# A one-layer block with dilated local attention and a gated ReLU network: the second norm only centred, its factor moved to the output rows, and some work moved between engines under a new order

## The chip, the cores and the metric

The kernel runs on one core of a Trainium2 chip. A core has a matrix engine (PE in the profile; its weight loads are PEld), a vector engine (DVE), a scalar engine (ACT), a general engine (POOL) and a synchronising engine that here only starts transfers (SP). PE writes its results into eight PSUM banks of 128 x 512 fp32; ACT or DVE must read a bank before PE can use it for something else. Transfers run on 16 shared DMA engines; SP, ACT and POOL only issue them.

The metric is the device time of one execution in microseconds (us). The kernel before takes 196.03 us (median of three runs, 195.43 to 196.18).

## The reference

The input x has 2048 rows of 512 numbers, in bf16. Two residual steps are computed:

```python
h  = x + attention(layernorm(x)) @ wo          # 32 heads of 16; each row sees itself and the rows
                                               # 2, 4, ..., 14 before it (8 places, dilation 2)
h2 = h + (relu(n @ W_gate) * (n @ W_up)) @ W_down      where n = layernorm(h)
```

The layer norm has no learned factor or offset: it subtracts the row's mean and divides by sqrt(variance + 1e-5). W_gate and W_up are 512 x 1376, W_down is 1376 x 512. ReLU of a row times a positive number is that number times the ReLU, so a positive factor s on a row n comes out of the gated product as s * s.

## The kernel before, in words

The 2048 rows are worked in four chunks of 512 (`tk` 0 to 3), each of four blocks of 128 rows (`j` or `n`). For every chunk the same steps are recorded as operations with an engine, a duration, the operations they depend on and the buffers they take or use:

- First norm (`layernorm` without `residual`): statistics on DVE (`xst`, `xag`), the factor on ACT (`xrl`, `xre`), normalised rows (`xxn`), then a transposition, since PE contracts over partitions: on PE with an ACT copy out of PSUM (`xtp`, `xte`), or, for the pairs of blocks named in `DMAT`, by a transposing DMA issued from SP (`xtd`, line 521).
- Projections (`qkv0` to `qkv11`, line 573): q, k and v in four tiles each, each four matmuls of 512 columns and one ACT copy out of PSUM (line 581). Six of chunk 0's are cut in smaller pieces (`qka` to `qke`) to start with the first rows.
- Scores: q times k at eight shifts, on DVE (`pr`, lines 624 and 639), in two halves `hf` of four shifts. PE sums over the 16 numbers of a head (`sc`, line 630: 16 matmuls that fill a quarter of the array each). For the halves in `PRE` DVE first adds the two products (`pa`, line 667) and PE does 8 matmuls instead of 16 (line 674). ACT takes the exponential (`ex`); the denominators come from PE (`den`), for the chunks in `DEN1` after DVE has added the two halves (`es`, line 720), else as two matmuls (line 708). ACT makes the reciprocal by Ln and Exp (`dl`, `dr`, lines 711 and 714) and DVE multiplies (`am`, line 732).
- SP spreads the weights over partitions with eight broadcasts per chunk (`bd`, line 748), DVE multiplies with v (`mu`, lines 780 and 795) and the eight places are added in three steps (`ta`, `tree`, line 783). The first and largest step is a DMA that adds, issued from POOL (line 823), for the pairs of chunk and tile in `DACC`, else it is done on DVE. `om` or the last step writes the attention output.
- Output projection `wo` (line 861). For the chunks in `RPE` (chunk 0) PE also adds x by a matmul with the identity (line 864) and ACT writes h and its row sum (`rs`, line 870); for the others DVE adds (`rs`, line 872).
- Second norm (`layernorm` with `residual`): DVE makes the negative mean (`hnm`, line 449); ACT makes the sum of squares (`hsq`, line 457), waits for all four blocks, then Ln and Exp (`hrl`, `hre`); only then DVE writes the normalised rows (`hxn`, line 503), which are transposed (`htp` and `hte`, or `htd` by DMA).
- The gated network: gate and up products (`mm`, line 934, and line 901 for the last 96 of 1376 columns), evicted by ACT (`ue`, `ge`) and multiplied on DVE (`gu`); the product with W_down (`dn`, line 984); its rows leave PSUM through ACT for chunks 0 and 1 (`o`, line 993), after which a DMA from POOL adds them to h (`oa`, line 1018), or through DVE, which adds h itself, for chunks 2 and 3 (`o`, line 997). SP stores the rows (`os`).

The order on every engine is fixed in the program. It comes from the list `RANK`: one rank for every operation, in the sequence in which they are recorded. Each engine, and with it the queue of transfers that it issues, works its own operations by rank; a planner (`Plan.order`) only merges these queues and picks buffers, with guessed durations. So an operation that waits holds up all that stands behind it on the same engine. Two weight loads are issued late: W_up after chunk 0's attention (`ldu`), W_down (`ldd`) after chunk 1's broadcasts. `DMAT`, `DACC`, `DEN1`, `PRE` and `RPE` are the lists that decide which engine does what.

Of the kernel before, what the change touches and what calls it, by code (L numbers as in the profile page):

```python
# [8 lines left out]
P = 128  # L9
# [47 lines left out]
]  # L57


class Op:  # L60
# [142 lines left out]
def kernel(  # L203
# [162 lines left out]

    PESUM = ()

    DACC = tuple((k, t) for k in range(3) for t in range(4))
    DAL = 5.5  # L370
    DAC2 = ()
    PRS, MUH = (0,), (0,)
# [698 lines left out]
```

## Time and profile before

| what | before |
|---|---|
| device time, median of three runs | 196.03 us (195.43 to 196.18) |
| profiled execution: time from its first to its last instruction | 193.3 us |
| PE busy | 188.5 us, 98% of the span |
| DVE busy | 149.1 us, 77% |
| ACT busy | 117.9 us, 61% |
| POOL busy | 18.1 us, 9% |
| granted PE clock | 1.000 |
| DMA | 24.61 MB, mean 127 GB/s |

The profiled execution's own time is its span, 193.3 us; the device times of the runs contain 2.7 us more at the median (196.03 - 193.3), which lies before the first and after the last instruction that the profile shows. Durations of instructions come from this one execution. Matmuls are pipelined: the duration of one is longer than the spacing of two, so times on PE are read from groups that follow each other without a break.

### The profile page before, as it was taken

The numbers are of one execution on the slowest core, as the hardware profiler recorded it, in microseconds if no ns is written. First come the engines' busy times: TensorE is split into PE (matmuls) and PEld (weight loads), VectorE is DVE, ScalarE is ACT, GpSimd is POOL, SyncE is SP. The second block draws the span as 40 slices with busy tenths as digits, with TensorE's granted clock in tenths as the row PEclk, the third lists the DMA queues.
The fourth block names the chain that finished last, engine by engine and source line by source line (L and its number), as shares of the span: only waits on it lengthen the run. The fifth ranks groups of instructions, "written<-read, shape, count | busy, mean of one in ns | idle before, by whom it ended". The sixth has DMA issues, their size and how long they took to land.

```text
span 193.3 us, 3095 instructions
## 1 busy us (share of the span) xinstructions
PE 188.5 (98%) x1141; PEld 98.0 (51%) x1141; DVE 149.1 (77%) x238; ACT 117.9 (61%) x245; POOL 18.1 (9%) x32
## 2 busy tenths in 40 slices
PE   7999998999999999999999999999999999999994
PEld 7985453554445443554455444444445445544543
DVE  6899999999899999999998847899965421314232
ACT  3589989887898667572465569505559611276300
POOL 3000003300400013200034101003000000000000
PEclk9999999999999999999999999999999999999999
DMA  6996284991257918947459987221400250170004
GB/s 204 326 353 279 59 191 97 201 201 22 79 213 178 301 33 163 191 84 165 106 111 188 190 171 159 59 54 32 80 0 0 54 136 4 27 244 0 0 4 135
DMA packets 25214, 24.61 MB, mean 127 GB/s; under 512 B 11408, under 2 KB 21488, under 8 KB 25200
## 3 DMA queue, kind: packets, MB, share of 16 engines
q1 hardware_dynamic: 22176, 16.13, 29.7%
q0 software_dynamic: 2304, 7.34, 20.5%
q10 hardware_dynamic: 720, 0.95, 1.5%
q8 instruction: 9, 0.15, 0.3%
q14 instruction: 5, 0.04, 0.1%
HBM read 8.42 MB, written 2.10 MB: 54 GB/s over the span
## 4 chain that ended last, share of the span: by engine, by line
PE 81%; DVE 7%; DMA 6%; ACT 1%; SPq 1%; issue 1%; ACTq 0%
PE bank L934 36%; PE bank L984 20%; PE bank L573 11%; PE bank L861 7%; DVE big L639 4%; PE bank L901 3%; PE bank L630 3%; DVE st L468 3%; DMA x_sm<-in_A_x_dram 2%; DMA wqk_sb<-in_A_wqkv_dram 2%; DMA quad<-row 1%; PE bank L532 1%; DMA big<-ex 1%; SPq L748 1%; ACT kT L581 0%
## 5 line engine op out<-in xcount | busy, mean ns | idle before, releaser
L934 PE MATMUL bank<-quad,wgu_sb 128*128 128x512 bf16 x320 | 71.9, 379 | 0.0
L934 PEld LDWEIGHTS <-wgu_sb 128*128 128x128 bf16 x320 | 31.0, 98 | 36.7 <-issue 0.8
L984 PE MATMUL bank<-wd_sb,gT 128*128 128x512 bf16 (+3 forms) x198 | 39.7, 355 | 0.0
L938 ACT CAST up_sb<-bank 128x512 bf16<-128x512 f32 x40 | 22.4, 592 | 20.7 <-PE bank L934 15.0
L941 ACT ACTIVATE gr<-bank 128x512 bf16<-128x512 f32 x40 | 23.2, 608 | 13.0 <-PE bank L934 9.8
L573 PE MATMUL bank<-quad,wqk_sb 128*128 128x512 bf16 (+2 forms) x176 | 29.9, 321 | 0.8 <-DMA quad<-row 0.8
L984 PEld LDWEIGHTS <-gT 128*128 128x128 bf16 (+1 forms) x198 | 18.4, 98 | 19.6 <-issue 0.4
L624 DVE TENSOR_TENSOR big<-quad,kT 128x4096 bf16<-128x4096 bf16 x12 | 27.2, 2283 | 0.1
L780 DVE TENSOR_TENSOR big<-big,vT 128x4096 bf16<-128x4096 bf16 x12 | 27.0, 2285 | 0.0
L962 DVE TENSOR_TENSOR gT<-gr,up_sb 128x1024 bf16<-128x1024 bf16 x20 | 13.7, 687 | 15.1 <-ACT gr L941 8.7
L573 PEld LDWEIGHTS <-wqk_sb 128*128 128x128 bf16 x176 | 17.1, 113 | 11.5 <-issue 1.4
L823 POOL DMA_DIRECT2D big<-big x12 | 10.5, 884 | 79.6 <-DVE big L780 47.2
L783 DVE TENSOR_TENSOR big<-big 128x1024 bf16<-128x1024 bf16 (+2 forms) x24 | 17.0, 729 | 0.6 <-DMA big<-big 0.5
L573 PE MATMUL bank<-quad,wv_sb 128*128 128x512 bf16 x64 | 15.9, 380 | 0.0
L861 PE MATMUL bank<-wo_sb,quad 128*128 128x512 bf16 x64 | 15.3, 379 | 0.0
L997 DVE TENSOR_TENSOR row<-x_sm,bank 128x512 bf16<-128x512 bf16 (+2 forms) x10 | 5.5, 578 | 12.4 <-PE bank L984 12.4
L457 ACT ACTIVATE row<-x_sm,mv 128x512 bf16<-128x512 bf16 x12 | 8.6, 715 | 4.5 <-DVE mv L449 4.5
L548 ACT COPY quad<-bank 128x1024 bf16<-128x1024 bf16 (+1 forms) x10 | 8.5, 890 | 3.5 <-PE bank L532 3.5
L872 DVE SCALAR_TENSOR_TENSOR x_sm<-x_sm,bank 128x512 bf16<-128x512 bf16 x12 | 8.2, 687 | 3.0 <-PE bank L861 3.0
L468 DVE BATCH_NORM_STATS2 st<-x_sm 128x6 f32<-128x512 bf16 x16 | 10.3, 678 | 0.2 <-DMA x_sm<-in_A_x_dram 0.2
L581 ACT CAST kT<-bank 128x512 bf16<-128x512 f32 x16 | 9.4, 600 | 1.4 <-PE bank L573 0.8
L573 PEld LDWEIGHTS <-wv_sb 128*128 128x128 bf16 x64 | 6.8, 114 | 6.4 <-issue 1.3
(77 smaller groups left out, 173.9 us busy)
## 6 DMA issues: line engine op xcount, KB each, us to landing
big<-big POOLq DMA_DIRECT2D x12, 512.0 KB, 5.3
big<-ex SPq DMA_DIRECT2D x32, 128.0 KB, 2.7
wgu_sb<-in_B_W_gate_dram SPq DMA_DIRECT2D x2, 688.0 KB, 9.9
wgu_sb<-in_B_W_up_dram SPq DMA_DIRECT2D x2, 688.0 KB, 4.7
wd_sb<-in_B_W_down_dram SPq DMA_DIRECT2D x2, 640.0 KB, 5.5
x_sm<-in_A_x_dram SPq DMA_DIRECT2D x2, 512.0 KB, 6.7
x_sm<-up_sb POOLq DMA_DIRECT2D x4, 256.0 KB, 4.5
out_dram<-x_sm SPq DMA_DIRECT2D x4, 256.0 KB, 2.3
```

The costliest lines, as they stand in the source:

```text
L468: V.bn_stats(out=st.t[:], in_=x_sm[:, tk * BPC + j, :])
L573: nc.tensor.matmul(mm.t[:, lo:hi], lhsT=wv_sb[:, dt, t:D:NT] if c == 2 else wqk_sb[:, dt, c * D + t:(c + 1) * D:NT], rhs=xnT.t[:, dt, lo:h ...
L624: V.tensor_tensor(out=pb.t[:].rearrange("p (t w) s -> p t w s", t=2), in0=q4, in1=k4, op=ALU.mult)
L780: V.tensor_tensor(out=mt.t[:], in0=ab.t[:], in1=v8, op=ALU.mult)
L783: V.tensor_tensor(out=mt.t[:, 0:n, :], in0=mt.t[:, 0:n, :], in1=mt.t[:, n:2 * n, :], op=ALU.add)
L823: nc.gpsimd.dma_start(mt.t[:, 0:4, :], mt.t[:, 4:8, :], accum_op=ALU.add)
L861: nc.tensor.matmul(od.t[:], lhsT=OT.t[:, t, j * P:(j + 1) * P], rhs=wo_sb[:, t, :], start=(t == 0), stop=(t == NT - 1 and tk not in RPE))
L934: nc.tensor.matmul(mm.t[:fs, lo:hi], lhsT=wgu_sb[:, dt, g, ft * P: ft * P + fs], rhs=hnT.t[:, dt, lo:hi], start=(dt == 0), stop=(dt == NT ...
L938: nc.scalar.copy(out=ub.t[:fs, i, :], in_=um.t[:fs, :])
L941: nc.scalar.activation(out=gr.t[:fs, i, :], in_=gm.t[:fs, :], func=ACT.Relu)
L962: V.tensor_tensor(out=gt.t[:fs, 0:n, :], in0=gr.t[:fs, 0:n, :], in1=ub.t[:fs, 0:n, :], op=ALU.mult)
L984: nc.tensor.matmul(od.t[:, c0:c1], lhsT=gts[ft].t[:fs, ft % 2, j * P:(j + 1) * P], rhs=wd_sb[:fs, ft, c0:c1], start=(ft == 0), stop=(ft == ...
```

## The change

The second norm is only centred. `hxn` writes h minus its mean as soon as the mean is known and no longer waits for `hsq`, `hrl` and `hre`. The exponent of `hre` becomes -1 instead of -1/2, so that it gives 1 / (variance + eps), the square of the former factor, in buffers of its own (`iv`). That number is applied to the rows at the end: in chunks 0 and 1 as the scale of ACT's copy out of PSUM, in chunks 2 and 3 as the scalar of DVE's multiply-and-add. The squares of `hsq`, of which only the sum is used, go to a scratch tile (`junk`).

Beside that: chunk 0's residual moves from PE and ACT to DVE (`RPE` is empty). Chunk 0's two halves of exponentials are added on DVE before the denominators (`DEN1`). Chunk 3's second half of scores is added in pairs on DVE as well (`PRE`). The first step of the sum over places becomes a DMA for three of chunk 3's four tiles (`DACC`). The second half of chunk 1's second norm is transposed by DMA too (`DMAT`). Ln of the denominators is written back into its PSUM bank instead of a buffer in SBUF. Once the last q and k projections are done, the tile of their weights serves as a sixth large buffer (`big`). All ranks are new, so that the order on every engine is another.

In the new order, by engine (`name.chunk`): SP's queue is `bd0.0 bd1.0 xtd.3 x4 ldu x2 bd1.1 bd0.1 ldd(second part).1 bd1.2 ldd(first part) bd0.2 gtd.0 htd.1 x4 ...`, where before it had `ldd` in both parts straight after chunk 1's broadcasts; PE does chunk 3's first projection straight after `den.0` and chunk 2's four `xtp` later, four `wo.1` before all `dn.0`, and `sc1.2` straight after `sc0.2` behind three `mm.0`.

```diff
-    DEN1 = (1, 2, 3)
+    DEN1 = (0, 1, 2, 3)
-    PRE = ((3,0),)
+    PRE = ((3,0),(3,1))
+    qkb = Buf(big_s)
+    wqk_f = wqk_sb[:].rearrange("p t (w s) -> p (t w) s", s=CS)
-    ln_s = slots(1, [P, CS], F32, "lnd")
+    iv_s = slots(4, [P, BPC], F32, "iv")
+    junk = sb.tile([P, CS], BF16, name="junk")
+    big_s.tiles.insert(0, wqk_f)
-    DACC = tuple((k, t) for k in range(3) for t in range(4))
+    DACC = tuple((k, t) for k in range(3) for t in range(4)) + ((3, 0), (3, 1), (3, 2))
-    DMAT = (('h',2,0),('h',2,2),('h',3,0),('h',3,2),('h',1,0),('x',3,0),('x',3,2))
+    DMAT = (('h',2,0),('h',2,2),('h',3,0),('h',3,2),('h',1,0),('h',1,2),('x',3,0),('x',3,2))
-    RPE, OPE = (0,), ()
+    RPE, POW = (), ()
...
-                        nc.scalar.activation(out=xn.t[:], in_=h.t[:] if h else x_sm[:, tk * BPC + j, :],
+                        nc.scalar.activation(out=junk[:], in_=h.t[:] if h else x_sm[:, tk * BPC + j, :],
                                              func=ACT.Square,
...
                 nc.scalar.activation(out=rs.t[:, lo:hi], in_=rs.t[:, lo:hi], func=ACT.Exp,
-                                     scale=-0.5)
+                                     scale=-1.0 if residual else -0.5)
...
+                elif residual:
+                    V.tensor_scalar(out=xn.t[:], in0=x, scalar1=mv.t[:, j, 0:1], scalar2=None, op0=ALU.add)
...
+                d, u = ([nms[j]], [mv]) if residual else ([e], [nb, rs] if on_act else [mv, rs])
...
-            nc.scalar.activation(out=ld.t[:], in_=dn.t[:], func=ACT.Ln)
+            nc.scalar.activation(out=dn.t[:], in_=dn.t[:], func=ACT.Ln)
...
-                    nc.scalar.copy(out=ob.t[:, j % 2, :], in_=od.t[:])
+                    nc.scalar.activation(out=ob.t[:, j % 2, :], in_=od.t[:], func=ACT.Identity, scale=iv.t[:, j:j + 1])
...
-                    V.tensor_tensor(out=ob.t[:, c0:c1], in0=x_sm[:, tk * BPC + j, c0:c1],
-                                    in1=od.t[:, c0:c1], op=ALU.add)
+                    V.scalar_tensor_tensor(out=ob.t[:, c0:c1], in0=od.t[:, c0:c1], scalar=iv.t[:, j:j + 1],
+                                           in1=x_sm[:, tk * BPC + j, c0:c1], op0=ALU.mult, op1=ALU.add)
```

More of the change, by code (lines that the diff above doesn't have):

```diff
@@ L416 @@
         wload[n] = []
+    wload["q"][0].take.append(qkb)
+    qkb.left += 1
     wb = Buf(bank_s)
@@ L491, in f_nb, with f_pw @@
                                        in1=rs.t[:, lo:hi], op0=ALU.mult, op1=ALU.mult)
-            l = add((ln + "rl" + gk, tk), "ACT", AS, f_ln, ag, pr, take=[rs], use=[sq or mv], lat=AL)
-            e = add((ln + "re" + gk, tk), "ACT", AS, f_ex, [l], pr, use=[rs], lat=AL)
-            if on_act:
+            def f_pw(lo=lo, hi=hi):
+                V.tensor_scalar(out=rs.t[:, lo:hi], in0=mv.t[:, lo:hi, 1], scalar1=EPS, scalar2=-0.5,
+                                op0=ALU.add, op1=ALU.pow)
+            if not residual and tk in POW:
+                e = add((ln + "pw" + gk, tk), "DVE", DSM, f_pw, ag, pr, take=[rs], use=[mv], lat=DL)
+            else:
+                l = add((ln + "rl" + gk, tk), "ACT", AS, f_ln, ag, pr, take=[rs], use=[sq or mv], lat=AL)
+                e = add((ln + "re" + gk, tk), "ACT", AS, f_ex, [l], pr, use=[rs], lat=AL)
+            if residual:
+                ivd.append(e)
+            elif on_act:
                 e = add((ln + "nb" + gk, tk), "DVE", DSM, f_nb, [e], pr, take=[nb], use=[mv, rs], lat=DL)
@@ L498, in f_xn @@
                 x = x_sm[:, tk * BPC + j, :]
-                if on_act:
+                if residual and on_act:
+                    nc.scalar.activation(out=xn.t[:], in_=x, func=ACT.Identity, bias=mv.t[:, j, 0:1], scale=1.0)
+                elif residual:
+                    V.tensor_scalar(out=xn.t[:], in0=x, scalar1=mv.t[:, j, 0:1], scalar2=None, op0=ALU.add)
+                elif on_act:
                     nc.scalar.activation(out=xn.t[:], in_=x, func=ACT.Identity,
@@ L708, in f_dn, with f_ld, f_rc @@
                 nc.tensor.matmul(dn.t[:], lhsT=(same if tk in EARLY else spread)[:], rhs=exs[hf].t[:], start=(hf == 0), stop=(hf == 1))
-        def f_ld(dn=dn, ld=ld):
-            nc.scalar.activation(out=ld.t[:], in_=dn.t[:], func=ACT.Ln)
-        def f_rc(ld=ld, rc=rc):
-            nc.scalar.activation(out=rc.t[:], in_=ld.t[:], func=ACT.Exp, scale=-1.0)
+        def f_ld(dn=dn):
+            nc.scalar.activation(out=dn.t[:], in_=dn.t[:], func=ACT.Ln)
+        def f_rc(dn=dn, rc=rc):
+            nc.scalar.activation(out=rc.t[:], in_=dn.t[:], func=ACT.Exp, scale=-1.0)
         if tk in DEN1:
@@ L725 @@
             b = add(("den", tk), "PE", 2 * MM, f_dn, exd, apr + 2, take=[dn], use=exs, lat=PEL)
-        b = add(("dl", tk), "ACT", A5, f_ld, [b], apr + 2, take=[ld], use=[dn], lat=AL)
-        rcd = add(("dr", tk), "ACT", A5, f_rc, [b], apr + 2, take=[rc], use=[ld], lat=AL)
+        b = add(("dl", tk), "ACT", A5, f_ld, [b], apr + 2, use=[dn], lat=AL)
+        rcd = add(("dr", tk), "ACT", A5, f_rc, [b], apr + 2, take=[rc], use=[dn], lat=AL)
         if tk in EARLY:
@@ L985, in f_dn, with f_o @@
                                      rhs=wd_sb[:fs, ft, c0:c1], start=(ft == 0),
[L986 to L991 removed]
+                                     stop=(ft == NFT - 1))
+            def f_o(j=j, c0=c0, c1=c1, od=od, ob=ob, tk=tk, iv=iv):
                 if tk in ODA:
[L993 to L998 removed]
+                    nc.scalar.activation(out=ob.t[:, j % 2, :], in_=od.t[:], func=ACT.Identity, scale=iv.t[:, j:j + 1])
+                else:
+                    V.scalar_tensor_tensor(out=ob.t[:, c0:c1], in0=od.t[:, c0:c1], scalar=iv.t[:, j:j + 1],
+                                           in1=x_sm[:, tk * BPC + j, c0:c1], op0=ALU.mult, op1=ALU.add)
             last = tk == NCK - 1 and n == len(parts) - 1
@@ L1006 @@
             for lo, hi in ((0, 8), (8, NFT)):
-                a = add(("dn%d" % n, tk), "PE", (hi - lo + (hi == NFT and tk in OPE)) * MM * share,
+                a = add(("dn%d" % n, tk), "PE", (hi - lo) * MM * share,
                         lambda lo=lo, hi=hi, f=f_dn: f(range(lo, hi)),
@@ L1011 @@
             if tk in ODA:
-                b = add(("o%d" % n, tk), "ACT", A5, f_o, [a], mb - 200, take=[ob], use=[od, ob], lat=AL)
+                b = add(("o%d" % n, tk), "ACT", A5 + 0.09, f_o, [a] + ivd, mb - 200, take=[ob], use=[od, ob, iv], lat=AL)
                 if j % 2 == 0:
@@ L1025 @@
                 continue
-            b = add(("o%d" % n, tk), "ACT" if tk in OPE else "DVE", D5 * share + (0.05 if share < 1 else 0), f_o, [a], mb - 200,
-                    take=[ob], use=[od], lat=DL)
+            b = add(("o%d" % n, tk), "DVE", D5 * share + (0.05 if share < 1 else 0), f_o, [a] + ivd, mb - 200,
+                    take=[ob], use=[od, iv], lat=DL)
             add(("os%d" % n, tk), "ACT" if last else "SP", 0.4, f_os, [b], mb + 6, use=[ob], lat=0.55, dq=(0.3, 0.4 * share))
```

42 lines of the change are left out of this document (17 added, 25 removed), and 76 rows, old and new, of the table RANK.

## The prediction

> **What bounds the kernel now.** I read the page, then the waits of PE, then the chain that ended last, then busy times by stretch, and last groups and timelines for single durations.
>
> ```profile
> span 193.3 us, 3095 instructions
> ...
> PE 188.5 (98%) x1141; PEld 98.0 (51%) x1141; DVE 149.1 (77%) x238; ACT 117.9 (61%) x245; POOL 18.1 (9%) x32
> ...
> PE   7999998999999999999999999999999999999994
> ```
>
> PE is busy in every slice. A busy PE need not work at its peak, so the waits say more. These are all waits of PE that the trace names:
>
> ```profile
> PE bank L422 <- DVE warm L322: 1.0, 1, 1.0
> PE bank L573 <- DMA quad<-row: 0.8, 1, 0.8
> ```
>
> The first is the start. The second is the only hole in the middle. The chain shows where it ends and what the work costs behind it (start, duration, what):
>
> ```profile
> 30.85 2.60 DMA quad<-row
> 33.45 0.14 issue
> 33.59 2.75 PE bank L573 x12
> ...
> 38.74 6.04 PE bank L573 x28
> 44.78 0.98 PE bank L630 x16
> ...
> 50.20 0.22 PE bank L864
> ...
> 60.37 0.89 PE bank L532 x16
> ...
> 73.57 0.55 PE bank L674 x8
> ...
> 81.34 0.66 PE bank L901 x8
> ...
> 87.84 3.45 PE bank L861 x16
> ...
> 180.87 9.59 PE bank L984 x66
> 190.46 0.02 issue
> 190.48 0.29 DVE row L997
> ```
>
> From 33.59 to 190.46 the chain holds nothing but matmuls, so there a matmul less is worth its spacing: 6.04 / 28 = 0.216 us for 512 columns, 0.89 / 16 = 0.056 for a transposition. A projection or a gate or up product (four matmuls) is 0.863, a score half 0.98, one added in pairs 0.55. After PE come 2.8 us of last row and store (193.3 - 190.5).
>
> DVE is nearly as full in the middle (columns: stretch, length, then busy time and count of PE, PEld, DVE, ACT, POOL):
>
> ```profile
> 34.00:60.00 26.00, 26.00 (x164) 12.65 (x163) 25.03 (x31) 22.19 (x49) 3.91 (x3) 1.00 0.62 142
> 60.00:80.00 20.00, 20.00 (x122) 9.27 (x121) 20.00 (x14) 12.71 (x24) 3.44 (x4) 1.00 0.72 174
> 80.00:100.00 20.00, 20.00 (x126) 10.04 (x124) 19.73 (x36) 11.83 (x27) 0.86 (x1) 1.00 0.56 117
> ```
>
> So PE sets the end as long as DVE hands it work in time: 64.8 us busy of 66 from 34 to 100.
>
> **What PE loses.** Behind 33.59: four identity matmuls of chunk 0's residual, 4 x 0.216 = 0.86; chunk 3's second score half, 0.98 - 0.55 = 0.43; eight transpositions of chunk 1, 8 x 0.056 = 0.45. Ahead of 33.59: one of chunk 0's two denominator matmuls, 0.22. The last is worth nothing: at the hole PE waits for the transposed rows of chunk 3, and these stand on SP's queue behind chunk 0's eight broadcasts, which start when DVE has ended its eight products, in both orders:
>
> ```profile
> 20.96 5.76 SPq L748 DMA_DIRECT2D big<-ex  x8
> ```
>
> Against that saving, chunk 2's first four transpositions, done ahead of that hole before, now stand behind it: +0.22. Sum: -0.86 - 0.43 - 0.45 + 0.22 = -1.52.
>
> In front of the hole the new order asks `sc0.0` after six of the eight products. By the row below these end at 12.82 + 5 x 1.147 = 18.6, and PE reaches it at about 18.1 (where `sc` stood before, less one transposition); the next, `sc1.0`, needs the eighth product, 20.85. I count 0.8 of new waits. PE had 0.8 to spare at the hole and gains 0.22, so they vanish in it; without that cover they would cost 0.6.
>
> ```profile
> 12.82 8.03 DVE L639 TENSOR_TENSOR big<-quad,kT 128x2048 bf16<-128x2048 bf16 x7
> ...
> 56.23 0.76 DVE L732 TENSOR_TENSOR ex<-ex,rec 128x512 bf16<-128x512 bf16 x2
> ...
> 60.47 6.68 DVE L624 TENSOR_TENSOR big<-quad,kT 128x4096 bf16<-128x4096 bf16 x3
> ...
> 69.28 4.50 DVE L780 TENSOR_TENSOR big<-big,vT 128x4096 bf16<-128x4096 bf16 x2
> ```
>
> **What the others gain and lose.** The groups, with busy time, mean ns of one, and the idle time ahead of them:
>
> ```profile
> L962 DVE TENSOR_TENSOR gT<-gr,up_sb 128x1024 bf16<-128x1024 bf16 x20 | 13.7, 687 | 15.1 <-ACT gr L941 8.7 <-ACT up_sb L938 6.3
> ...
> L500 ACT ACTIVATE row<-x_sm,nb,rs 128x512 bf16<-128x512 bf16 x12 | 9.4, 817 | 0.3 <-DVE nb L489 0.3
> ...
> L872 DVE SCALAR_TENSOR_TENSOR x_sm<-x_sm,bank 128x512 bf16<-128x512 bf16 x12 | 8.2, 687 | 3.0 <-PE bank L861 3.0
> ...
> L783 DVE TENSOR_TENSOR big<-big 128x2048 bf16<-128x2048 bf16 x4 | 4.8, 1220 | 0.0
> ...
> L993 ACT CAST up_sb<-bank 128x512 bf16<-128x512 f32 x8 | 4.4, 599 | 7.4 <-PE bank L984 7.4
> ...
> L870 ACT ACTIVATE x_sm<-bank 128x512 bf16<-128x512 f32 x4 | 2.4, 594 | 0.3 <-PE bank L864 0.3
> ...
> L667 DVE TENSOR_TENSOR big<-big,big 128x4096 bf16<-128x4096 bf16 x1 | 2.3, 2281 | 0.0
> ...
> L720 DVE TENSOR_TENSOR row<-ex,ex 128x512 bf16<-128x512 bf16 x3 | 1.2, 417 | 0.0
> ```
>
> DVE: +4 x 0.69 (chunk 0's residual), +0.42 (`es.0`), +2.28 (pairs), -3 x 1.22 (three first steps of chunk 3 sent to POOL), together +1.8; the output rows that now multiply and add cost what line 872 does, 0.69, and lie beside PE's work but for the last one, 0.29 long. The +3.2 of chunk 0 come early, in the full stretch; the relief comes behind 120. ACT loses 4 x 0.6 and scales eight output rows, 0.60 each now; the new price lies between the same (a scale is free) and the 0.82 of line 500, which scales from SBUF, so 0 to 1.8 in all. I take 0.8, half-way; any of it is hidden in its 39% of idle time, 7.4 us of it ahead of those very rows. Ln into PSUM I price at nothing: same instruction, same input; its bank is held one operation longer. The shorter norm (squares, Ln and Exp out of the path) I also price at nothing: PE waited for no norm after the hole. It pays for DVE's extra work.
>
> **Where the new order can stall: chunk 1.** On PE, from 33.59: 24 projections 20.7, four `xtp` 0.9, two scores 1.96, four `wo.0` 3.45, `den` 0.22, four `htp` 0.89, so the first gate product stands at 61.7, and with 0.1 lost at each change to the scores 61.9. Then 20 gate and up products and two short ones (17.3 + 1.3), two scores, `den.2`: `wo.1` at 82.7, and behind its four `dn.0` at 86.2.
>
> DVE: `am0.1` ended at 56.99 before. Now it has 0.42 and 2.76 and the four centred rows (1.3) more ahead of it, one product (2.2) less, and a wait of 0.65 gone: 58.6. Then four score products (6.68 / 3 = 2.2 each), four products with v (2.2 each), `es.2`, one `gu`, one first sum and `am1.2`: 17.6 + 0.4 + 0.7 + 0.6 + 0.4 = 19.7, which gives `am1.2` at 78.3. Two `gu` and the other sums of chunk 1, 4.4, give the last attention row at 82.7: exactly when PE wants it. Each us that DVE is later here, PE waits. I take 0, half-way between a margin of 0.3 and a wait of 0.3.
>
> At `am1.2` hangs a step that was moved on SP's queue: the first part of W_down, issued before with its second part at 62, now stands behind `bd1.2`, which waits for `am1.2`.
>
> ```profile
> 57.07 5.12 SPq L748 DMA_DIRECT2D big<-ex  x8
> ...
> 62.24 1.22 SPq L304 DMA_DIRECT2D wd_sb<-in_B_W_down_dram  x2
> ...
> 109.51 4.25 SPq L748 DMA_DIRECT2D big<-ex  x4
> ```
>
> ```profile
> big<-big POOLq DMA_DIRECT2D x12, 512.0 KB, 5.3
> ...
> wd_sb<-in_B_W_down_dram SPq DMA_DIRECT2D x2, 640.0 KB, 5.5
> ```
>
> Four broadcasts take 5.12 / 2 = 2.6, so W_down's part goes out at 80.9 and lands at 86.4, against `dn.0` at 86.2: 0.2 late. Lower bound 0 (it lands earlier with the queues empty); upper bound 1.9, if the broadcasts take the 4.25 of the row at 109.51, which ran beside adding transfers. Chunk 1's last adding transfer is issued at about 75.2 and lands at 80.5, so most of its time lies ahead. I take 0.3.
>
> The four transposing DMAs of chunk 1 are issued from 89 on, 1.3 apart, after `rs.1`, and land at 95.6; PE needs them at 96.4. Hidden; the cover is the 9.5 us of `dn.0`. Other handoffs that I added up the same way (chunk 2's output projection at 115, its norm at 128, chunk 3's at 145 and 159) have 0.4 to 3 us.
>
> **Sum.** 193.3 - 1.52 + 0.3 = 192.1, which is -1.2. The profiled execution lies 2.7 below the median, all of it outside the span, so -1.2 is taken from 196.03: 194.8 us.
>
> **A rule against the value of a matmul less.** Four matmuls of 512 columns follow each other every 0.216 us here. The Trainium skill, "TensorE: Matmul & The Clock Gate", section Back-to-back issue gap, states about 131 ns per matmul of 512 columns and 81 ns for 128 as what a real kernel sustains. By it the residual and the transpositions would be worth an estimated 0.52 and 0.65 in place of 0.86 and 0.45, nearly the same sum. The trace disagrees with both figures (0.216 and 0.056), and I go by the trace.
>
> **The rivals.**
>
> (a) The new waits eat most of it: W_down lands 1.9 late, or DVE is 0.5 late at `wo.1` and W_down 1.0 late. About 193.3 - 1.5 + 1.6 = 193.4, so 196.1. For it: two handoffs of margin near zero at 82.7 and 86.2. Against: the order before had as full a DVE and PE did not wait once behind 33.59. Chance 0.22.
>
> (b) On the other side, DVE becomes the bound between 50 and 83: it gets 3.2 us there while it is already 98% busy, and PE has filler only to 82.7. Price: one to one. It decides against the kernel (over +0.5%, 197.0) from 2.2 us of lateness on, beside W_down's 0.3: 197.3 at 2.5. Against: the sums above must be 2.5 short over 25 us of DVE time. Chance 0.11.
>
> (c) Chunk 3's adding transfers hold up DVE. They stand behind the output additions `oa.1` on POOL, which wait for ACT's rows at 129 and 130; landing 5.3 after issue plus the shared time of the output addition, the tree starts at about 137, `gu3.2` behind it at 140, and PE, with all eight banks full, would stop at 141.5. If each landing came 2.2 later, 1 us is lost: 195.8. For 2.2: POOL's issue held by the DVE product that runs. Against: POOL issued one in 0.86 inside the DVE row at 69.28, as here:
>
> ```profile
> 71.87 0.86 POOL L823 DMA_DIRECT2D big<-big  x1 [21.29 <-DVE big L780]
> ```
>
> The Trainium skill, "SBUF — State Buffer", section A bandwidth-pool intuition that's wrong, states that a DMA issued from POOL waits for its descriptors until a DVE instruction that holds the shared port has ended. The row shows no such wait for these products. Chance 0.05.
>
> **How the numbers follow.** Likeliest: PE's saving with small waits, 0.62, 194.8; its own range is 194.3 (no wait) to 195.0. (a) 0.22, (b) 0.11, (c) 0.05. The measurement tells about 0.5%, 1.0 us, from no change: faster is below 195.05, slower above 197.0. Faster 0.62, same 0.27 (a and c), slower 0.11. The range reaches from 194.0 to 196.6: it holds the likeliest, (a) and (c), and leaves out (b) and the tails.
>
> **What would show it.** Right: no line 864 on PE; a pair of scores more in line 674's counterpart; PE's only waits at 18 to 33 and near 83 to 87; PE's last matmul at 189.2. W_down's wait would stand as PE waiting for a DMA into `wd_sb`, (b) as PE waiting for attention rows (`quad` from DVE) at 83, (c) as DVE waiting for `big<-big` at 132 to 140 and PE for ACT at 141. The forecast is wrong if a wait stands at another handoff, or if the hole at 33 ends much later, since all behind it shifts with it.

## The result, and the profile after

The changed kernel takes 195.19 us (median of 16 runs, 193.94 to 196.07), the kernel before 195.62 (16 runs, 195.06 to 196.18): ratio 0.9966, 95% interval 0.995 to 0.9982. Two later comparisons gave 0.9952 and 0.9962. So it is faster by 0.34%, about 0.7 us (the two medians alone differ by 0.43), where 1.2 us were forecast, and less than the 0.5% above which I had called it faster. The profiled execution took 195.59, 0.4 above the median. For 212 runs of the kernels below both the time and the span of the same execution were measured: the time is 1.7 to 2.25 us longer than the span. So the profile of the kernel before, with a span of 193.3, is of an execution of some 195.0 to 195.5, and not all of the 2.7 us that I put outside the span lies there.

First the page of the changed kernel: its span, and busy time, share and instructions of each engine.

```profile
span 193.6 us, 3051 instructions
...
PE 185.8 (96%) x1120; PEld 95.9 (50%) x1120; DVE 150.2 (78%) x245; ACT 115.8 (60%) x236; POOL 22.9 (12%) x35
```

PE is busy for 2.7 us less than before, and yet the span of this execution is 0.3 longer. The waits of PE (total, times, longest):

```profile
PE bank L550 <- DVE row L521: 2.2, 2, 1.9
PE bank L429 <- DVE warm L327: 1.0, 1, 1.0
PE bank L591 <- DMA quad<-row: 0.9, 1, 0.9
PE bank L723 <- DVE row L738: 0.4, 1, 0.4
```

All four lie ahead of or in the hole. None of the waits that I had feared behind it is there. The chain (start, duration, what) shows the same handoffs as the forecast, all later by one amount:

```profile
32.40 2.61 DMA quad<-row
35.01 0.14 issue
35.15 5.34 PE bank L591 x24
...
63.65 2.59 PE bank L952 x12
...
84.40 3.45 PE bank L879 x16
87.85 8.86 PE bank L1002 x41
```

The hole ends at 35.15, before at 33.59: 1.56 later. Less this, the first gate product stands at 62.09 (forecast 61.9), `wo.1` at 82.84 (82.7) and `dn.0` at 86.29 (86.2). The part of W_down that `dn.0` needs landed at 87.48, 0.37 ahead of it. At the end, the timeline of the changed kernel:

```profile
183.80 6.49 PE L1002 MATMUL bank<-wd_sb,gT 128*128 128x512 bf16 x47
...
187.29 3.81 SPq L1016 DMA_DIRECT2D out_dram<-row  x6
188.44 1.41 DVE L1010 SCALAR_TENSOR_TENSOR row<-bank,iv,x_sm 128x512 bf16<-128x512 f32 x2 [0.52 <-PE bank L1002]
190.13 0.61 DVE L1010 SCALAR_TENSOR_TENSOR row<-bank,iv,x_sm 128x128 bf16<-128x128 f32 x2 [0.28 <-DMA out_dram<-row]
190.51 0.35 ACTq L1016 DMA_DIRECT2D out_dram<-row  x1
```

PE's last matmul ends at 183.80 + 6.49 = 190.29, so from the hole's end PE needs 155.14; before it was 190.45 - 33.59 = 156.86. PE's saving is 1.72. But the last rows of DVE wait 0.28 for a store (the bracket in their row), and the span ends 3.3 behind the last matmul, where it was 2.8. So 1.72 were won between two points, and 1.56 lost ahead of them and 0.46 behind.

### The profile page after: what moved, and what is told of

Read it like the earlier page. It is cut to its first block, busy times and chain, and to the rows that moved or that the text cites. A ratio compares the mean times of both kernels' runs of the same rounds, so it can differ in the third digit from the quotient of the medians.

```text
span 193.6 us, 3051 instructions
## 1 busy us (share of the span) xinstructions
PE 185.8 (96%) x1120; PEld 95.9 (50%) x1120; DVE 150.2 (78%) x245; ACT 115.8 (60%) x236; POOL 22.9 (12%) x35
## 4 chain that ended last, share of the span: by engine, by line
PE 82%; DMA 7%; ACT 5%; issue 2%; DVE 1%; SPq 0%; DVEq 0%
PE bank L952 35%; PE bank L591 16%; PE bank L1002 15%; PE bank L879 7%; PE bank L648 3%; DMA x_sm<-in_A_x_dram 3%; DMA quad<-row 3%; PE bank L919 3%; PE bank L550 2%; ACT vT L599 1%; DMA out_dram<-row 1%; ACT junk L462 1%; ACT row L518 1%; DVE row L1010 1%; ACT gr L959 1%
## 5 line engine op out<-in xcount | busy, mean ns | idle before, releaser
L642 DVE TENSOR_TENSOR big<-quad,kT 128x4096 bf16<-128x4096 bf16 x11 | 24.9, 2289 | 0.1
L798 DVE TENSOR_TENSOR big<-big,vT 128x4096 bf16<-128x4096 bf16 x10 | 22.5, 2289 | 0.5 <-DMA big<-ex 0.5
L841 POOL DMA_DIRECT2D big<-big x13 | 12.5, 985 | 63.8 <-DVE nb L494 31.6
L1008 ACT ACTIVATE up_sb<-bank,iv 128x512 bf16<-128x512 f32 x8 | 5.1, 684 | 16.3 <-PE bank L1002 16.3
L801 DVE TENSOR_TENSOR big<-big 128x1024 bf16<-128x1024 bf16 (+2 forms) x19 | 12.1, 660 | 3.4 <-DMA big<-big 3.3
L890 DVE SCALAR_TENSOR_TENSOR x_sm<-x_sm,bank 128x512 bf16<-128x512 bf16 x16 | 10.7, 683 | 3.0 <-PE bank L879 3.0
L462 ACT ACTIVATE junk<-x_sm,mv 128x512 bf16<-128x512 bf16 x16 | 11.7, 731 | 1.5 <-DVE mv L456 1.5
L813 DVE TENSOR_TENSOR big<-big,vT 128x2048 bf16<-128x2048 bf16 x8 | 9.3, 1219 | 1.4 <-DMA big<-ex 1.4
L599 ACT CAST quad<-bank 128x512 bf16<-128x512 f32 x16 | 9.1, 590 | 2.1 <-PE bank L591 2.1
L518 ACT ACTIVATE row<-x_sm,nb,rs 128x512 bf16<-128x512 bf16 x12 | 9.8, 815 | 0.3 <-DVE nb L494 0.3
```

Of the source, the lines that this page charges most:

```text
L462: nc.scalar.activation(out=junk[:], in_=h.t[:] if h else x_sm[:, tk * BPC + j, :], func=ACT.Square, bias=mv.t[:, j, 0:1], scale=1.0, accum ...
L642: V.tensor_tensor(out=pb.t[:].rearrange("p (t w) s -> p t w s", t=2), in0=q4, in1=k4, op=ALU.mult)
L798: V.tensor_tensor(out=mt.t[:], in0=ab.t[:], in1=v8, op=ALU.mult)
L801: V.tensor_tensor(out=mt.t[:, 0:n, :], in0=mt.t[:, 0:n, :], in1=mt.t[:, n:2 * n, :], op=ALU.add)
L841: nc.gpsimd.dma_start(mt.t[:, 0:4, :], mt.t[:, 4:8, :], accum_op=ALU.add)
```

## The experiments

The first theories were these. I: the input's blocks land at other times in each execution, and the hole follows. S: the new start order, that of the first operations on DVE and ACT, makes the hole later by 0.5 at any landing. W: waits behind the hole. F came up after the first four runs and is told there.

**The same two kernels again** (labels "changed again" and "before again" in the table below).

> The changed kernel as it is, once more. Theory I (input): in its profiled execution the input rows merely landed late (fourth block at 7.19 us, last block of chunk 1 at 10.30, against 5.91 and 9.40 before), and everything up to the hole at 33 us shifted with them. Then the end of the hole, where the first projection of chunk 3 starts on PE (35.15 there), follows the landing of chunk 1's last block in any execution: landing near 9.4 gives a hole that ends near 33.8 and a span near 191.9. Theory S (start order): the new order of the first rows on DVE, in which block 1 is written only after block 3 has landed, costs about 0.5 us at any landing: the hole ends at 34.3 or later even with a landing at 9.4. Both: PE has no wait over 0.3 us behind the hole.

> The kernel before, once more, for its landings. Theory I: the landing of chunk 1's last input block (9.40 us before) and the end of the hole on PE (33.59) move from execution to execution by 0.5 us or more, and together. Theory S: they stay within 0.2 us, so that the later hole belongs to the new order.

The changed kernel took 194.81 (7 runs), ratio 0.9952 (0.9927 to 0.9977); the one run of the kernel before 194.81, which is low for it (22 runs, 194.63 to 196.38, median 195.64). In both profiles the last input block of chunk 1, for whose statistics DVE's first score products wait, landed at about the same time, 9.19 and 9.15 us, so theory I does not explain what differs. SP's timeline, changed again:

```profile
20.83 6.65 SPq L766 DMA_DIRECT2D big<-ex  x8
27.58 5.25 SPq L539 DMA_TRANSPOSE quad<-row  x4
```

and before again:

```profile
20.70 5.69 SPq L748 DMA_DIRECT2D big<-ex  x8
26.49 5.25 SPq L521 DMA_TRANSPOSE quad<-row  x4
```

SP starts together, but needs 0.96 more to issue the same eight broadcasts. One of the issues takes 1.97 in place of some 0.6 (1.08 before). The first broadcast lands 4.19 after its issue, in the kernel before 3.26. What stands between: a transfer of another kind among the broadcasts' packets. The transfers that started between 22.2 and 22.4 in this profile of the changed kernel (packets, MB, share of 16 engines):

```profile
q1 hardware_dynamic: 20, 0.02, 66.6%
q8 instruction: 1, 0.02, 47.5%
```

The program itself is fetched by such transfers, nine of 16 KB on this queue. Counting PE's weight loads (one for each matmul) in the traces, the second one comes after 212 to 222 of them and the ninth after 1095 to 1100, in every kernel run here; so I take them for PE's, and their time follows PE's progress. Those between scatter more, the fourth from 459 to 497. Each takes about 1 us (0.9 to 1.6). In the kernel before the second one starts at 21.74 and 21.95, ahead of the broadcasts' first packets; in the changed kernel at 22.23 and 23.28, among them. The ninth starts at 184.05 and 184.32 before, where nothing else is under way, and at 187.06 and 187.90 in the changed kernel, where the last rows are stored: it has 21 matmuls with 21 weight loads less, so the same count comes nearer to the end. Changed again, the end of its timeline:

```profile
183.72 5.63 PE L1002 MATMUL bank<-wd_sb,gT 128*128 128x512 bf16 x43
...
186.34 4.42 SPq L1016 DMA_DIRECT2D out_dram<-row  x6
187.50 1.41 DVE L1010 SCALAR_TENSOR_TENSOR row<-bank,iv,x_sm 128x512 bf16<-128x512 f32 x2 [0.52 <-PE bank L1002]
189.80 0.61 DVE L1010 SCALAR_TENSOR_TENSOR row<-bank,iv,x_sm 128x128 bf16<-128x128 f32 x2 [0.89 <-DMA out_dram<-row]
190.18 0.35 ACTq L1016 DMA_DIRECT2D out_dram<-row  x1
```

before again:

```profile
183.70 6.49 PE L984 MATMUL bank<-wd_sb,gT 128*128 128x512 bf16 x47
...
187.33 3.19 SPq L1003 DMA_DIRECT2D out_dram<-row  x6
...
190.23 0.29 DVE L997 TENSOR_TENSOR row<-x_sm,bank 128x128 bf16<-128x128 bf16 x1 [0.33 <-PE bank L984]
190.55 0.36 ACTq L1003 DMA_DIRECT2D out_dram<-row  x1
```

PE ended at 189.35, 0.84 ahead of the kernel before (190.19), close to the forecast (189.2). But DVE's last rows waited 0.89 for the first of the stores, whose row buffer they need: it landed 3.33 after its issue, before 1.71. This is **theory F**: two of PE's instruction transfers now meet transfers on which the hole and the end depend, the second one later than before and the ninth for the first time.

**Start order.** The changed kernel with the old order of DVE's, ACT's and PE's first operations, by permuting ranks:

```diff
+_order(19, 20, 27, 28, 23, 35, 31, 36, 42, 43, 34, 39, 46)   # DVE: xst0 xag0 xst1 xag1 xxn0 xst2 xxn1 xag2 xst3 ...
+_order(21, 22, 29, 30, 26, 37, 38, 44, 45, 41, 48)           # ACT
+_order(24, 25, 32, 33, 67, 61, 77, 72, 55, 68, 73, 40, 78, 47, 74)   # PE
```

> The changed kernel, with the first rows in the order of the kernel before: on DVE block 1 is written ahead of block 3's statistics, ACT's factors to match, on PE the transpositions of blocks 2 and 3 behind the first pieces of the projections. Theory S: the hole ends about 0.5 us earlier than in the changed kernel at the same landing, and the median falls by 0.5 us (ratio to before about 0.994). Theory I: no difference, median within 0.2 us of the changed kernel's (0.9966).

195.2 us, ratio 0.9974 (0.995 to 0.9997): no gain over the changed kernel in the same comparison (0.9952). The first broadcast goes out 11.65 after chunk 1's last block landed, with the new start order 11.63 and 11.64, before 11.56 and 11.55. S falls; its price is 0.1 at most.

**Chunk 0's second four broadcasts from POOL**, so that SP reaches the transposing DMAs earlier:

```diff
-    BCD = {(0,0):"SSSS",(0,1):"SSSS", ...
+    BCD = {(0,0):"SSSS",(0,1):"PPPP", ...
```

> The changed kernel, with the second four of chunk 0's eight broadcasts issued by POOL instead of SP, so that chunk 3's four transposing transfers stand behind four issues less on SP's queue. If SP's queue sets the end of the hole (my prediction's reading), the transfers go out up to 2.6 us earlier, bounded by ACT's rows, and the hole ends 1.0 to 1.5 us earlier: ratio to before about 0.991. If ACT's rows set it, it ends 0.3 us earlier at most: 0.995. If broadcasts from POOL are slow, DVE waits for chunk 0's second half of weights and nothing is won.

The hole was all but gone (it ended at 33.18 with a block landing of 9.32), but from there PE needed 156.6, 1.45 more than the changed kernel, in waits of 0.3 and less: 196.03 us, ratio 1.0017 (0.9987 to 1.0047). Chunk 1's first broadcast went out 25.1 after the hole's end, in the changed kernel 24.0, so that the earlier end of the hole was lost again; which of the waits comes from POOL's queue I did not separate.

**Moving the instruction transfers.** Three kernels change how many instructions PE has ahead of the transfers. The first has 20 more pairs of weight load and matmul in the warming group at the start (line 429), the second is the kernel before with 5 pairs fewer there, and the third has 20 tiny matmuls in the hole, so that only the transfers behind it move:

```diff
# changed kernel, 40 instructions more
-    NWARM, NFILL = 46, (8, 0, 0)
+    NWARM, NFILL = 66, (8, 0, 0)
-            nc.tensor.matmul(wb.t[:, 0:P], lhsT=warm[:], rhs=warm[:], start=True, stop=True)
+            nc.tensor.matmul(wb.t[:, 0:88], lhsT=warm[:, 0:P], rhs=warm[:, 0:88], start=True, stop=True)
# kernel before, 10 instructions fewer
+    NWARM, NFILL = 41, (8, 0, 0)
# changed kernel, 40 instructions more in the hole (in f_dn)
+            for _ in range(20 if tk == 0 else 0):
+                nc.tensor.matmul(dn.t[:, 0:4], lhsT=warm[:], rhs=warm[:, 0:4], start=True, stop=True)
```

> The changed kernel with 66 warming matmuls of 88 columns in place of 46 of 128, so 40 more TensorE instructions (a weight load and a matmul each) ahead of everything, in about the same time. Theory F (one of the 16 KB instruction transfers, which come at a fixed count of TensorE's instructions, falls among chunk 0's first broadcasts at 22.2 to 23.3 us, and the last one among the last output rows at 187.1 to 187.9): both fall earlier, near 20.7 and near 183, where the DMA engines have nothing to do. The first broadcast lands some 2.9 us after its issue and not 3.9 to 4.2, no broadcast's issue takes over 1.2 us, the hole ends 0.6 to 0.9 earlier at the same landing of chunk 1's last block; the first of the last output rows lands 1.7 after its issue and not 2.7 to 3.3, the end is another 0.5 to 1.0 earlier. Sum 1.1 to 1.8: 193.3 to 193.9 us, ratio 0.988 to 0.991. Theory I (only the input blocks land at other times from one execution to the next): as the changed kernel, ratio 0.995 to 0.997.

> The kernel before with 41 warming matmuls in place of 46, so 10 TensorE instructions fewer ahead of everything and nothing else changed. Theory F: the instruction transfer that started at 21.74 and 21.95 us, ahead of the first broadcast's data, starts about 1 us later, among them; the first broadcast lands 3.9 to 4.3 us after its issue instead of 3.3, one broadcast's issue takes 1.5 to 2.0 instead of 1.1, the hole ends 0.4 to 0.9 later; the last transfer of instructions comes at 185.3 instead of 184.3, still ahead of the output rows. 196.0 to 196.5 us, ratio 1.002 to 1.005. Theory I: no change, 0.999 to 1.001.

> The changed kernel with 20 matmuls of 4 columns put into the hole, ahead of den.0 (line 723), where TensorE waits anyway; their result is overwritten. So the second instruction transfer stays where it was and the last one comes 40 TensorE instructions earlier, near 183 us. Theory F: the broadcasts and the hole as in the changed kernel (first broadcast 3.9 to 4.2 us after its issue), the first of the last output rows lands 1.7 us after its issue and not 2.7 to 3.3; only the end is earlier, by 0.5 to 1.0: ratio 0.991 to 0.993. Should the matmuls hold up den.0, up to 0.3 of that is lost. Theory I: no change, 0.995 to 0.997.

> The changed kernel once more, beside the three variants: ratio 0.995 to 0.997. Theory F: in its profile the first broadcast again lands 1.2 us after the end of the instruction transfer near 23 us, and the first of the last output rows 1.2 us after the end of the one near 188 us, whenever chunk 1's last block lands. Theory I: both transfers take as long as in the kernel before once that block lands as early as 9.2 to 9.4 us.

Times: 195.44, ratio 0.9997 (0.9979 to 1.0015); 195.7, ratio 1.0003 (0.9986 to 1.002); 196.35, ratio 1.0021 (0.9994 to 1.0047); the changed kernel beside them 195.02, ratio 0.9962 (0.9944 to 0.998). By the times F's sums fail for all three. By the traces the transfers that moved did what F says, and the sums missed the other seven transfers. In us from the span's start:

| profile | block lands | first broadcast issued | 2nd instruction transfer ends | first broadcast lands | hole ends | PE's last matmul ends | span |
|---|---|---|---|---|---|---|---|
| before | 9.40 | 20.96 | 23.08 | 24.30 | 33.59 | 190.45 | 193.3 |
| before again | 9.15 | 20.70 | 22.74 | 23.96 | 33.31 | 190.19 | 193.0 |
| changed | 10.30 | 21.93 | 24.64 | 25.87 | 35.15 | 190.29 | 193.6 |
| changed again | 9.19 | 20.83 | 23.75 | 25.02 | 34.20 | 189.35 | 193.2 |
| changed, third | 10.33 | 23.23 | 26.26 | 25.87 | 35.95 | 191.09 | 195.1 |
| old start order | 10.32 | 21.97 | 25.09 | 26.31 | 34.82 | 189.96 | 193.5 |
| 40 more | 10.04 | 23.11 | 23.00 | 25.76 | 35.24 | 192.06 | 195.3 |
| 40 more in the hole | 10.15 | 21.81 | 24.03 | 25.40 | 34.40 | 191.48 | 194.7 |
| 14 more (below) | 8.97 | 20.74 | 22.95 | 24.17 | 33.28 | 188.61 | 191.8 |
| 14 more, other buffers (below) | 10.18 | 23.77 | 26.19 | 27.46 | 36.52 | 192.12 | 195.3 |

These single executions are not all typical of their kernels. The third of the changed kernel took 197.27 (median of its runs 195.02), 40 more 197.32 (195.44), 40 more in the hole 196.69 (196.35), 14 more 193.93 (194.99), and the last one 197.34 (194.7).

Where the first broadcast is still under way when the transfer ends, it lands 1.22 to 1.37 after that end; this holds for the kernel before too. Where the transfer was over before the first issue (40 more), the first broadcast landed 2.65 after its issue, SP issued all eight in 5.21, and the hole ended 12.13 after the first issue, in the changed kernel 13.2 and 13.4 (12.7 in its third profile), before 12.6. The first of the last stores landed 1.74 and 1.73 after issue in the two kernels with 40 more. So far as expected. But with 40 more, the fourth transfer, at 68.4 in the changed kernel, started at 64.94 and 63.62, among chunk 1's broadcasts: one issued at 63.15 landed at 67.19, 4.0 later, in the changed kernel 2.6 (63.04 to 65.62). DVE waits for it, SP's queue behind DVE, and PE in the end. PE's waits behind the hole, 40 more:

```profile
PE bank L952 <- ACT up_sb L956: 0.5, 1, 0.5
PE bank L879 <- DVE quad L835: 0.2, 1, 0.2
PE bank L919 <- ACT up_sb L956: 0.2, 1, 0.2
```

and 40 more in the hole:

```profile
PE bank L921 <- ACT up_sb L958: 0.5, 1, 0.5
PE bank L1004 <- DMA wd_sb<-in_B_W_down_dram: 0.4, 1, 0.4
PE bank L954 <- ACT up_sb L958: 0.4, 1, 0.4
```

From the hole's end PE needs 156.82 and 157.08 here, 1.7 and 1.9 more than the 155.15 of the changed kernel. The view counts a wait from the end of the matmul before, 0.38 after its start, where without a wait the next one starts after 0.22; so each of these waits costs 0.16 more than it shows, and the three make 1.4 and 1.8. In the first of the two something else came on top: the first broadcast went out 13.1 after the block's landing, since PE's granted clock (the number ahead of the DMA share) was 0.57 while it made chunk 0's projections:

```profile
8.00:12.00 4.00, 3.51 (x33) 3.43 (x34) 3.81 (x9) 1.67 (x4) 0.00 (x0) 0.57 0.93 295
```

The kernel before with 10 instructions fewer tells nothing: its transfer started only 0.14 later, not 1 us, as PE runs the small matmuls of the scores at that place. In the third profile of the changed kernel the granted clock fell in the same way, so that the broadcasts went out later (12.9 after the block's landing) and met the transfer otherwise than expected: it ended at 26.26, after the first broadcast's landing; the second landed 1.25 after it, and the first of the last stores 1.22 after the ninth transfer, 3.5 after its issue.

**A smaller shift.** 14 more instructions, which moves the transfers by some 1 us and should leave the fourth one behind chunk 1's broadcasts; and the same with the last two pieces written to buffers that are free:

```diff
-    NWARM, NFILL = 46, (8, 0, 0)
+    NWARM, NFILL = 53, (8, 0, 0)
-            nc.tensor.matmul(wb.t[:, 0:P], lhsT=warm[:], rhs=warm[:], start=True, stop=True)
+            nc.tensor.matmul(wb.t[:, 0:111], lhsT=warm[:, 0:P], rhs=warm[:, 0:111], start=True, stop=True)
# second kernel, beside that; row_of takes one half of an up buffer
-                ob = Buf(o_s)
+                ob = Buf(up_s if n > BPC else o_s)
```

> The changed kernel with 53 warming matmuls of 111 columns in place of 46 of 128: 14 more TensorE instructions ahead of everything, so that the instruction transfers come about 1 us earlier and not 2 to 3, and the fourth one (68.4 us, 64.9 in the run with 40 more, where it fell among chunk 1's broadcasts) stays behind those broadcasts, near 67. Theory F: the second transfer starts 0.3 to 0.8 us after the first broadcast's issue (1.35 to 1.9 in the changed kernel), the first broadcast lands 2.8 to 3.3 after its issue, the hole ends 24.1 to 24.4 after the landing of chunk 1's last block (24.85 to 25.6 in the changed kernel, 24.2 before); the ninth ends 1 us earlier, the first of the last output rows lands 1.7 to 2.2 after its issue, and the span ends 3.2 to 3.4 behind TensorE's last matmul instead of 3.3 to 4.0; no TensorE wait behind the hole, 155.1 from the hole's end to the last matmul. Sum 0.8 to 1.5 below the changed kernel: ratio 0.988 to 0.992. Theory I (only landings of the input differ): 0.995 to 0.997.

> As the one before, and the last two pieces of the last output row go into a buffer of the up products, so that their VectorE rows need not wait until an earlier row has been sent out. Theory F: if the ninth instruction transfer is clear of the output rows, this brings 0 to 0.2 (ratio 0.987 to 0.992); if it still meets them, the last row follows TensorE's last matmul at once all the same, and the span ends 3.0 to 3.3 behind it. Theory I: 0.994 to 0.997, as only the wait of 0.3 to 0.9 ahead of the last rows is gone.

The first: 194.99, ratio 0.9949 (0.9927 to 0.9971). SP's timeline, and then the end of PE's and DVE's:

```profile
20.74 5.87 SPq L766 DMA_DIRECT2D big<-ex  x8
26.71 5.22 SPq L539 DMA_TRANSPOSE quad<-row  x4
...
183.63 4.98 PE L1002 MATMUL bank<-wd_sb,gT 96*128 96x512 bf16 x40
...
188.65 0.35 DVE L1010 SCALAR_TENSOR_TENSOR row<-bank,iv,x_sm 128x128 bf16<-128x128 f32 x1 [0.22 <-PE bank L1002]
```

The profile is close to what was expected: the hole ends 24.31 after the block's landing (24.16 and 24.19 before, 24.85 and 25.01 changed), PE needs 155.33 from there, the last row follows the last matmul at once, and the span ends 3.2 behind it. Two things are off. The first broadcast landed 3.4 after its issue, where 2.8 to 3.3 were expected. And the fourth transfer came at 64.04 and not near 67; the last of chunk 1's broadcasts was then 0.5 from its landing and came 2.7 after its issue, as usual, so that PE did not wait. The median is not as expected: 0.9949 instead of 0.988 to 0.992; the profiled execution was 1.1 shorter than the median. The second kernel: 194.7, ratio 0.9926 (0.9897 to 0.9955), within what was expected but for 0.0006; it is the fastest of all, though its interval overlaps those of the changed kernel. In its profile PE waited for nothing behind the hole and the span ended 3.2 behind the last matmul, as expected. So the traces show the two meetings and what each costs there, but moving them brings less at the median than the profiles say. What the median keeps is open; the landing of the input (8.97 to 10.33 in these profiles) may be part of it, and so may the clock (last section).

**Two of the parts.** The kernel before with chunk 0's residual on DVE, in its old order; and the same with the second norm only centred as well:

```diff
-    RPE, OPE = (0,), ()
+    RPE, OPE = (), ()
# second kernel, beside that: the edits of the change at hre, hxn, hsq, the output rows and Ln of the denominators
```

> The kernel before with one part of the change: chunk 0's residual is added by VectorE (four rows of 0.69) and not by four identity matmuls on TensorE; order of operations as before. By the prediction's sum: TensorE needs 0.86 less behind the hole, 156.0 from the hole's end to its last matmul (156.87 before), and the time is 194.7 to 195.2, ratio 0.9955 to 0.998, if VectorE, 2.8 us fuller between 45 and 60, still hands on in time. By rival (b), VectorE the bound there: TensorE waits behind line 861 or 934 for up to 2 us, ratio 1.000 to 1.010. Theory F adds: eight TensorE instructions fewer behind the hole move the ninth instruction transfer from 184.3 to about 184.3 as well (0.9 us of work less, 0.9 us later by count), clear of the output rows; the span ends 2.8 behind TensorE's last matmul, as before. Theory I: the landing of chunk 1's last block is again 9.1 to 9.4, or, if it is chance, may be near 10.3 as in the changed kernel.

> The kernel before with two parts of the change, in its own order of operations: chunk 0's residual on VectorE (as in the run with that part alone, which took 198.0 us, ratio 1.0105) and the second norm only centred, its factor put on the output rows. By the prediction's sentence that the shorter norm pays for VectorE's extra work: TensorE's waits at the norm of chunk 0 near 62 us (1.4 in the run with the residual alone) shrink to under 0.5, 155.9 to 156.8 from the hole's end to TensorE's last matmul, ratio 0.998 to 1.003. By the rival, that only the new order of VectorE's work makes room for the four rows: VectorE has no wait for ScalarE's Exp ahead of these rows in the old order, so the centred rows start where the normalised ones started (61.7 us there), the waits stay, 158.0 to 158.5 from the hole's end, ratio 1.008 to 1.013.

198.0 us, ratio 1.0105 (1.0077 to 1.0134), and 197.55, ratio 1.0085 (1.0059 to 1.0111): slower by 1%. PE's waits behind the hole, residual alone:

```profile
PE bank L532 <- DVE row L503: 1.3, 1, 1.3
PE bank L705 <- DVE row L720: 0.6, 1, 0.6
```

residual and centring:

```profile
PE bank L535 <- DVE row L499: 1.2, 1, 1.2
PE bank L708 <- DVE row L723: 1.1, 1, 1.1
```

DVE's timeline in the second:

```profile
59.69 2.28 DVE L627 TENSOR_TENSOR big<-quad,kT 128x4096 bf16<-128x4096 bf16 x1
61.88 1.14 DVE L499 TENSOR_SCALAR row<-x_sm,mv 128x512 bf16<-128x512 bf16 x4
```

The centred rows (line 499) start at 61.88, the normalised ones of the residual alone at 61.68. They stand behind score products on DVE's queue, not behind the Exp that the centring removes, and PE needs 158.3 and 158.6 from the hole's end, 1.4 and 1.7 more than before. Here score products (at 52.13, 56.08 and 59.69 in the second kernel) stand among the rows of the residual and ahead of the centred ones. In the changed kernel no score product stands among the four rows of the residual and the four centred rows; two come before and three behind them (first residual row, last centred row, products):

```profile
54.82 0.68 DVE L890 SCALAR_TENSOR_TENSOR x_sm<-x_sm,bank 128x512 bf16<-128x512 bf16 x1
...
59.03 0.35 DVE L516 TENSOR_SCALAR row<-x_sm,mv 128x512 bf16<-128x512 bf16 x1
...
59.62 6.69 DVE L642 TENSOR_TENSOR big<-quad,kT 128x4096 bf16<-128x4096 bf16 x3
```

So by themselves, in the old order, two of the change's parts cost 1%; together with the other parts in the new order PE had no wait here. The new order without the other parts, and the other parts without the order, were not run.

## Why the prediction was half right

The time lies in the forecast range, but the case that came is the one called "same" (chance 0.27), not the likeliest. That the time is in the range is in part luck: two terms that I had put at nothing cost 1.1 and 1.8 us in the first two profiles, a larger saving and a stall that did not come gave 0.5 back, and the range is wide. By steps:

- **PE's saving, -1.52:** right, 1.72 in three profiles of the changed order (155.14 and 155.15 in the changed kernel, 155.14 with the old start order, from the hole's end). Spacings summed from the traces give the other 0.2: the four identity matmuls took 0.96 and not 0.86, and the scores 0.55 less and not 0.43.
- **The waits ahead of the hole, 0.8 counted at the scores:** none there. PE waited 2.2, 0.7 and 1.8 for the first norm's rows instead (line 521), which it did not do before; in the first two profiles the hole hides that, and the third is told in the last section.
- **The stall at chunk 1, +0.3 taken:** none. W_down's part landed 0.37 ahead of `dn.0` and no wait stands at `wo.1`. That both margins are near zero was right: with chunk 1's last broadcasts 1 us later (40 more in the hole) PE waited 0.4 for `wd_sb`, and at 141 for ACT, the place of rival (c).
- **The hole, taken to end at the same time in both orders:** this step failed. The first issue follows the block's landing as before (11.6), but from it to the hole's end it is 13.2 and 13.4 instead of 12.6 (12.7 in the third profile, 12.85 with the old start order), because PE's second instruction transfer ended later after that issue, among the broadcasts. What such a meeting costs varies, 0.1 to 0.8 in these four, and not with the lateness of the transfer alone: with the old start order it ended latest, 3.1 after the issue. The profiled execution lost another 0.9 to a late input block; that differs from execution to execution, 9.19 and 10.30 in the same kernel.
- **"After PE come 2.8 us of last row and store":** this step failed too; 3.3, 3.9 and 4.0 in the changed kernel, 3.5 with the old start order. With the ninth transfer out of the way (40 more) it is still 3.2. In thirteen of the fourteen profiles the span ends 1.3 to 1.4 behind the landing of SP's last store (1.6 with broadcasts from POOL), and PE now computes the piece last that SP stores. An order that ends with ACT's store was not tried.
- **The sum:** -1.72, with +0.6 and +0.8 at the hole and +0.5 and +1.0 at the end, gives -0.6 and +0.1 in the two profiles of the changed kernel, with the landing left out. The ratios say -0.7 and -0.9. These two executions lie 0.4 above their medians and the second one of the kernel before lies 0.8 below its own, so the first agrees and the second does not settle it.
- **ACT's output rows:** 684 ns against 599 for the copy, between the bounds; **DVE:** busy 1.1 more, where I had counted 1.8.
- **"It pays for DVE's extra work":** wrong as put. In the old order the centring paid nothing that could be measured.
- **Rival (b)**, DVE as the bound, did not come in the changed kernel, but its price is real: it is what the residual costs in the old order, where two waits for DVE (2.2, with 0.16 added to each) less the matmuls saved (0.96) make most of the 1.4 above. Rival (a), new waits behind the hole, has about the right size for what was lost and the wrong place.

## What to carry to other kernels

A sum over the busiest engine is only as good as the two points between which it is taken: check what sets its first matmul behind the last hole and what follows its last one, and whether these stay. When a change alters how many instructions an engine runs, look where its instruction transfers fall, since a few instructions can move one of them into, or out of, a transfer that somebody waits for. Price an edit together with the order that it runs in: two parts of this change cost 1% in the old order, while the whole of it, in an order made for it, gained 0.3%. And ask of a profile how far its execution lies from the median before you add up its rows.

## What the runs showed of the hardware

- Transfers of 16 KB of instructions come at nearly the same counts of PE's work (the second after 212 to 222 weight loads, the ninth after 1095 to 1100), take 0.9 to 1.6 us each, and go with a delay of what else is queued: a broadcast of 128 KB that was under way landed 1.22 to 1.37 after the end of one, in eleven profiles, instead of 2.65 after its issue, and one of SP's next issues stretched from 0.6 to as much as 1.97 meanwhile. The Trainium skill, "Runtime: NRT & Kernel Launch", section Instruction fetch mechanics, says that each sequencer fetches blocks of 16 KiB, 256 instructions, over a DMA queue of its own while it executes, at a cost that is mostly hidden. It is hidden from PE here, which showed no wait at these places, but not from the transfers beside it.
- PE's granted clock fell to 0.50 for 3.4 us in three of the fourteen profiles: 40 more (8.15 to 11.56), the changed kernel's third (8.61 to 12.02) and 14 more with other buffers (8.68 to 12.09). The first broadcast then went out 12.9 to 13.6 after the block's landing instead of 11.55 to 12.0. In all three PE had waited for the first norm's rows of the new start order (1.8 to 2.6 in two waits), but in the changed kernel's first profile the clock stayed at 1.00 behind a wait of 1.9. The Trainium skill, "TensorE: Matmul & The Clock Gate", section What's actually happening, says that the clock is set by windows that run freely; the trace agrees in that the length of the wait alone did not decide. A mean granted clock of 0.991 or less stands at 7 of the 100 runs of the changed kernel and its variants and at none of 112 of the kernel before and its variants (lowest 0.998).
- The last input block of chunk 1 landed between 8.97 and 10.33 us. The hole's end moved with it: 0.25 and 0.28 in the two profiles of the kernel before, 1.11 and 0.95 in the first two of the changed kernel.
